# Sliding-window attention and a gated FFN: keys and queries loaded four tokens to a row over all partitions, heads paired two apart

## The chip, the cores and the metric

One core of a Trainium2 chip runs the whole program. The metric is the device time in microseconds (us) of one execution. Engines are called as the profile calls them: PE is TensorE's matmuls, PEld its weight loads, DVE is VectorE, ACT is ScalarE, POOL is GpSimd, SP is SyncE.

## The reference

Attention with sinks and a window over 4 batches, 8 heads, 768 tokens and a head size of 64, followed by a gated FFN over the 3072 tokens:

```python
scores = scale * np.matmul(q, k.transpose(0, 1, 3, 2))
keep = is_sink | in_window            # the first 4 keys, or 0 <= row - col < 128
a = softmax(np.where(keep, scores, -1e9))
attn_out = np.matmul(a, v)
x = attn_out.transpose(0, 2, 1, 3).reshape(B * S, H * D)     # 3072 x 512
g = x @ w_gate                                               # 512 x 1536
out = (g * sigmoid(g) * (x @ w_val)) @ w_out                 # 1536 x 512
```

Inputs and output are float32; the kernel works in bfloat16 with float32 accumulation.

## The kernel before

Tokens are cut into 12 groups of 256, numbered `g`; three groups make a batch, so groups 0, 1 and 2 are batch 0. A group goes through a fixed row of steps: its keys and queries are turned so that the head size lies on the partitions (`kT`, `qT`, two heads stacked on 128 partitions as a pair `p`, the half called `w` or `h`); `step_S` makes scores and their exponentials into the tile `e`; `step_K` and `step_sinks` do the sink keys; `step_PV` multiplies with the values and normalises; `step_X` turns the result for the FFN (`xT`). The FFN runs over eight blocks of 256 or 512 tokens, as `gate` units (a gate projection, a value projection, 6 or 12 per block) and `down` units. The order of all work is written out by hand: the lists given to `weave` put attention steps of later groups between the FFN units of earlier ones. All engines run their own instructions in the program's order.

The keys and queries reach `kT` and `qT` in different ways. Group 0 is cast and turned in `pair_T` (line 572) from the tile `x0`, which holds two tokens of one head in a row. Heads 0 to 3 come as float32 through SP and ACT into the tiles `st` (line 175) and are cast by DVE and ACT (`cast`, lines 562 and 564); heads 4 to 7 come through POOL, cast on the way (line 186). Group 1 comes by `load_rows` (line 100) into `rows`, four tokens of a head in a row, the first head of each pair on partitions 0 to 63 and the second on 64 to 127, and is turned by `step_T` (line 226). Groups 2 and 3 come by `load_nat` (line 111) with one token on each partition and are turned by `step_TN` (line 241). The later groups are turned by DMA (`xbar`).

A turn in `pair_T` and `step_T` is a matmul whose stationary operand is a piece of rows and whose moving operand is the identity `ident`; the outputs for the tokens of one place `r` in the row go to every second or every fourth column of the PSUM tile `pt`.

At the start PE runs 14 matmuls on zeros (`fill`, line 556), then `pair_T(0)`, `pair_T(1)`, `pair_S(0)`, `pair_S(1)`, `pair_T(2)`, `pair_T(3)`, `pair_S(2)`, `pair_S(3)`, the four `step_T` of group 1, `step_PV` of group 0, `step_S` of group 1, and the first gate unit. The loads of group 1, the values and the first gate weights wait in the POOL queue behind those of line 186 (lines 100, 122, 133); POOL also makes `tq` and `tk` (lines 187, 189), from which DVE builds `ident` (line 200). The four `step_TN` of group 2 stand in two FFN units, two in each, at about 25 and 27 us.

`step_vsb` puts the sink values of 8 heads on the partitions where the sink scores of the heads will lie (`load_sinks` gives the order) and masks them with `diag_h`.

Of the kernel before, what the change touches and what calls it, by code (L numbers as in the profile page):

```python
# [7 lines left out]
FP32 = mybir.dt.float32  # L8
BF16 = mybir.dt.bfloat16
AF = mybir.ActivationFunctionType  # L10
ALU = mybir.AluOpType
# [3 lines left out]
def kernel(  # L15
# [12 lines left out]
    nc = tc.nc  # L28
    P = 128
    B, H, S, D = q.shape  # L30
    NS = int(n_sink)
# [7 lines left out]
    NP2 = H // 2  # L39
    GC = S // 256  # L40
# [12 lines left out]
    def pool(name, bufs, psum=False):  # L53
        if psum:
            return ctx.enter_context(
                tc.tile_pool(name=name, bufs=bufs, space=bass.MemoryType.PSUM))
        return ctx.enter_context(tc.tile_pool(name=name, bufs=bufs))

    const = pool("const", 1)
    wpool = pool("wpool", 1)  # L60
    rowp = pool("rowp", 3)
# [16 lines left out]
    def bank(shape, dtype, name):  # L78
        return psum.tile(shape, dtype, tag="b", name=name)


    rows, nats, vas = {}, {}, {}

    def by_rows(src, b, w, pairs, t0):

        hs = slice(2 * pairs.start + w, 2 * pairs.stop, 2)
        return src[b, hs, t0:t0 + 256].rearrange("p (m r) d -> m p (r d)", r=4)

    ALL = slice(0, NP2)

    def new_rows(g):
        rows[g] = rowp.tile([P, 2, NP2, 4 * D], BF16, tag="rows", name="rows")
        return rows[g]

    def load_rows(g, i):
        b, c = divmod(g, GC)
        if g not in rows:
            new_rows(g)
        for w in range(2):
            nc.gpsimd.dma_start(  # L100
                rows[g][64 * w:64 * (w + 1), i],
                by_rows((k, q)[i], b, w, ALL, c * 256))

    def load_nat(g):
        b, c = divmod(g, GC)
# [38 lines left out]
    ident = const.tile([P, P], BF16)  # L144
    mask = const.tile([P, 2, 256], BF16)
    mask0 = const.tile([P, 2, 256], BF16)
    diag_h = const.tile([P, 4], BF16)
    vcf = const.tile([P, 1, D + 1], FP32)
    vcl = const.tile([P, B - 1, D + 1], FP32)
# [15 lines left out]

    def by_two(src, h0, n=4):
        return src[0, h0:h0 + n, 0:256].rearrange("h (m r) d -> m h (r d)", r=2)

    x0 = const.tile([P, 2, H, 2 * D], BF16)
    st = [rowp.tile([P, H, 2 * D], FP32, tag="rows", name="st") for _ in range(2)]
    for h0 in (0, 2):
        for i, eng in ((0, nc.sync), (1, nc.scalar)):
            eng.dma_start(st[i][:, h0:h0 + 2], by_two((k, q)[i], h0, 2))
    nc.scalar.activation(warmed, one, AF.Exp)

    def load_sinks(t, b0, b1):
        for h in range(H):
            r = 32 * (h // 4) + NS * (h % 4)  # L180
            nc.sync.dma_start(
                t[r:r + NS, :, 0:D], v[b0:b1, h, 0:NS].rearrange("b s d -> s b d"))

    load_sinks(vcf, 0, 1)
    for i in range(2):
        nc.gpsimd.dma_start(x0[:, i, 4:8], by_two((k, q)[i], 4))
    nc.gpsimd.iota(tq, [[1, P]], base=0, channel_multiplier=0,
                   allow_small_or_imprecise_dtypes=True)
    nc.gpsimd.iota(tk, [[0, 1]], base=0, channel_multiplier=1,
# [13 lines left out]
    kTs, qTs, es_t, e_t, xns, xTs = {}, {}, {}, {}, {}, {}  # L203
# [7 lines left out]
    def new_T(b):  # L211
        if b not in kTs:
            kTs[b] = kqtp.tile([P, NP2, S], BF16, tag="kT", name="kT")
            qTs[b] = kqtp.tile([P, NP2, S], BF16, tag="qT", name="qT")

    def step_T(g, i, p2, evict=None):
        b, c = divmod(g, GC)
        new_T(b)
        x = rows[g]
        pt = bank([P, 2, 256], FP32, "pt")  # L220
        for pp in range(2):
            p = 2 * p2 + pp
            for r in range(4):
                for w in range(2):
                    h = slice(64 * w, 64 * (w + 1))
                    nc.tensor.matmul(  # L226
                        pt[h, pp, r:256:4], x[h, i, p, r * D:(r + 1) * D],
                        ident[h, h], start=True, stop=True, skip_group_check=True)
        dst = (kTs, qTs)[i][b][:, 2 * p2:2 * p2 + 2, c * 256:(c + 1) * 256]
        if (evict or ("a", "v")[i]) == "a":  # L230
            nc.scalar.copy(out=dst, in_=pt)
        else:
            nc.vector.tensor_copy(out=dst, in_=pt)

    def step_TN(g, i, j, evict="av"):

        b, c = divmod(g, GC)
        new_T(b)
        pt = bank([P, NP2, P], BF16, "pn")
        for p in range(NP2):  # L240
            nc.tensor.transpose(pt[:, p], nats[g][:, i, j, p * P:(p + 1) * P], ident)  # L241
        t0 = c * 256 + j * P
        dst = (kTs, qTs)[i][b][:, :, t0:t0 + P]
        if evict[i] == "a":
            nc.scalar.copy(out=dst, in_=pt)
        else:
            nc.vector.tensor_copy(out=dst, in_=pt)
# [15 lines left out]

    def step_vsb(b):
        vsb = const.tile([P, 4, D + 1], BF16, tag=f"vsb{b}", name="vsb")
        (nc.vector if b else nc.gpsimd).tensor_tensor(
            vsb,
            (vcl[:, b - 1:b] if b else vcf).broadcast_to([P, 4, D + 1]),
            diag_h.rearrange("q (h o) -> q h o", o=1).broadcast_to([P, 4, D + 1]),
            op=ALU.mult)  # L270
        vsbs.append(vsb)

    def step_S(g, p2):
# [50 lines left out]
    def step_sinks(g):  # L324

        b, c = divmod(g, GC)
        for j in range(2):
            for hh in range(2):
                r = slice(32 * (2 * j + hh), 32 * (2 * j + hh + 1))
                pos[j, hh] = bank([P, 4, D + 1], FP32, "o")  # L330
                nc.tensor.matmul(pos[j, hh], es_t[g][r], vsbs[b][r], start=True,  # L331
                                 stop=False, skip_group_check=True)

    def step_PV(g, j, hh, norm="v"):
        b, c = divmod(g, GC)
        t = 2 * c + j
        if hh == 0:
            xns[g, j] = xnp.tile([P, DM], BF16, tag="xn", name="xn")
        if c > 0 and j == hh == 0:
            step_sinks(g)  # L340
        po = pos.pop((j, hh)) if c > 0 else bank([P, 4, D + 1], FP32, "o")
        mms = []
        for hq in range(4):
            h = 4 * hh + hq
            if t > 0:
                vp = vas[g][:, 0, h, 0:D + 1] if j else vas[g - 1][:, 1, h, 0:D + 1]
                mms.append((po[:, hq], e_t[g][:, h, 256 * j:256 * j + P], vp))
            mms.append((po[:, hq], e_t[g][:, h, 256 * j + P:256 * (j + 1)],
                        vas[g][:, j, h, 0:D + 1]))
        for i, (o, l, r) in enumerate(mms):  # L350
            nc.tensor.matmul(o, l, r, start=(c == 0 and i == 0),  # L351
                             stop=(i == len(mms) - 1),
                             skip_group_check=True)

        xn = xns[g, j][:, 256 * hh:256 * (hh + 1)].rearrange("p (h d) -> p h d", h=4)

        def dve():
            rcp = smallp.tile([P, 4, 1], FP32, tag="rcp", name="rcp")
            nc.vector.reciprocal(rcp, po[:, :, D:D + 1])  # L359
            if norm == "a":  # L360
                for hq in range(4):
                    nc.scalar.activation(  # L362
                        xn[:, hq], po[:, hq, 0:D], AF.Copy, scale=rcp[:, hq])
            else:
                nc.vector.tensor_tensor(  # L365
                    xn, po[:, :, 0:D], rcp.broadcast_to([P, 4, D]), op=ALU.mult)
        if norm == "a":
            dve()
        else:
            later.append(dve)  # L370
# [186 lines left out]
                             stop=True, skip_group_check=True)  # L557

    def cast(i, p):
        h = slice(2 * p, 2 * p + 2)  # L560
        if i == 0:
            nc.vector.tensor_copy(out=x0[:, i, h], in_=st[i][:, h])
        else:
            nc.scalar.copy(out=x0[:, i, h], in_=st[i][:, h])

    def pair_T(p):
        new_T(0)
        for i, dst in ((0, kTs[0]), (1, qTs[0])):
            pt = bank([P, 256], FP32, "pt")
            for r in range(2):  # L570
                for w in range(2):
                    nc.tensor.matmul(  # L572
                        pt[64 * w:64 * (w + 1), r:256:2],
                        x0[:, i, 2 * p + w, r * D:(r + 1) * D], ident,
                        start=True, stop=True, skip_group_check=True)
            if p < 2 and i == 0:
                nc.scalar.copy(out=dst[:, p, 0:256], in_=pt)
            else:
                nc.vector.tensor_copy(out=dst[:, p, 0:256], in_=pt)
# [29 lines left out]
    cast(1, 1)  # L609
    nc.vector.tensor_scalar(mask[:, :, P:2 * P], tq2, tk, None, op0=ALU.is_ge)  # L610
    pair_T(0)
    pair_T(1)
    nc.vector.tensor_scalar(sk, tk, float(NS), None, op0=ALU.is_lt)
# [130 lines left out]
```

## Time and profile before

| | |
|---|---|
| median of 3 runs | 238.30 us (237.76, 238.30, 238.68) |
| profiled execution, first to last instruction (span) | 235.8 us |
| mean granted clock over the span | 0.999 |
| PE busy | 229.0 us (97%), 1867 matmuls |
| DVE, ACT, POOL busy | 157.7, 113.6, 74.9 us |
| DMA | 27.62 MB, 108743 packets |

The profile gives the span as the profiled execution's own time; the timed runs are 2.0 to 2.9 us longer, for what lies around the span. In the profile, "L572" is line 572 of the kernel, "pt<-ident,x" an instruction that writes the tile `pt` from `ident` and `x`, and "x16" says how many were merged in one row. A matmul's time in a row includes its way through the array; what a series costs is read from start to start.

### The profile page before, as it was taken

Reading aid. Unit: us, or ns where it says so; the run is one execution under the profiler, and the core shown is the slowest. Engines: PE = TensorE matmul, PEld = TensorE weight load, DVE = VectorE, ACT = ScalarE, POOL = GpSimd, SP = SyncE. Lnnn points to the kernel's source line nnn. Section 1 sums busy time; section 2 is a strip of 40 time slices with the busy share of each in tenths; the row PEclk is TensorE's granted clock in tenths of the full one; section 3 lists DMA queues with packets and bytes.
Section 4 is the critical chain, followed back from the end, with each engine's and each line's share of the span. In section 5 each row is a group of like instructions: output and inputs, shape, how many; then the busy total and the mean of one; then the engine's idle time right before and its main releaser. Section 6 shows DMA issues by size and latency. Waiting matters only on the chain.

```text
span 235.8 us, 4879 instructions
## 1 busy us (share of the span) xinstructions
PE 229.0 (97%) x1867; PEld 127.7 (54%) x1893; DVE 157.7 (67%) x333; ACT 113.6 (48%) x235; POOL 74.9 (32%) x100
## 2 busy tenths in 40 slices
PE   8999999999999999999999999999999999999994
PEld 5768545795555654444445444445444445488443
DVE  4998888768660988950888970698960598877000
ACT  4884495367453826423836522755522653333221
POOL 8995874724403209105325350080000000000000
PEclk9999999999999999999999999999999999999999
DMA  8999999995995929957989997599414100200132
GB/s 138 165 183 176 182 200 204 159 147 81 166 227 164 148 47 88 156 112 160 137 114 133 137 132 185 126 89 101 81 25 150 50 3 0 45 4 0 48 131 91
DMA packets 108743, 27.62 MB, mean 117 GB/s; under 512 B 95792, under 2 KB 105776, under 8 KB 108720
## 3 DMA queue, kind: packets, MB, share of 16 engines
q0 software_dynamic: 76640, 13.90, 76.4%
q1 hardware_dynamic: 30672, 11.58, 25.4%
q10 hardware_dynamic: 1408, 1.84, 2.5%
q8 instruction: 15, 0.25, 0.5%
q14 instruction: 8, 0.07, 0.1%
HBM read 28.34 MB, written 6.29 MB: 147 GB/s over the span
## 4 chain that ended last, share of the span: by engine, by line
PE 93%; DVE 3%; ACT 1%; issue 1%; DVEq 0%; ACTq 0%
PE pv L416 26%; PE pd L496 26%; PE pg L416 26%; PE o L351 4%; PE s L288 4%; PE w L556 1%; DVE xn L365 1%; PE pt L226 1%; PE o L331 1%; PE pt L572 1%; PE pn L241 1%; PE pk L316 1%; ACT th L436 1%; DVE rcp L359 0%; ACT xn L362 0%
## 5 line engine op out<-in xcount | busy, mean ns | idle before, releaser
L444 DVE SCALAR_TENSOR_TENSOR u<-th,pg 128x512 bf16<-128x512 f32 x72 | 49.2, 683 | 39.2 <-ACT th L436 39.2
L416 PE MATMUL pg<-xT,wg 128*128 128x512 bf16 (+1 forms) x353 | 73.5, 336 | 0.7
L436 ACT ACTIVATE th<-pg 128x512 f32<-128x512 f32 x72 | 43.5, 604 | 63.0 <-PE pg L416 58.2
L416 PE MATMUL pv<-xT,wv 128*128 128x512 bf16 (+1 forms) x349 | 72.9, 336 | 0.6 <-ACT e L295 0.2
L496 PE MATMUL pd<-wo,ht 128*128 128x512 bf16 (+2 forms) x292 | 64.5, 371 | 0.5 <-issue 0.2
L416 PEld LDWEIGHTS <-wg 128*128 128x128 bf16 x360 | 35.0, 98 | 27.9 <-issue 0.4
L455 DVE TENSOR_TENSOR ht<-u,pv 128x512 bf16<-128x512 bf16 x62 | 42.7, 688 | 9.4 <-PE pv L416 2.5
L295 ACT ACTIVATE e<-s 128x512 bf16<-128x512 f32 (+1 forms) x88 | 42.8, 581 | 3.9 <-PE s L288 3.7
L496 PEld LDWEIGHTS <-ht 128*128 128x128 bf16 x300 | 27.9, 98 | 30.3 <-issue 0.3
L416 PEld LDWEIGHTS <-wv 128*128 128x128 bf16 x360 | 32.1, 97 | 20.4 <-issue 1.6
L501 ACT ACTIVATE ot<-pd 128x512 f32<-128x512 f32 (+1 forms) x24 | 14.3, 596 | 46.7 <-PE pd L496 40.7
L111 POOL DMA_DIRECT2D nat<-in_k_dram x20 | 17.7, 890 | 39.7 <-DMA qT<-nat 35.8
L300 DVE TENSOR_TENSOR e<-e,mask 128x1024 bf16<-128x1024 bf16 (+1 forms) x44 | 27.2, 653 | 3.7 <-ACT e L295 3.7
L122 POOL DMA_DIRECT2D va<-in_v_dram x24 | 21.5, 919 | 5.5 <-DMA wo<-in_moe_w_out_dram 2.5
L365 DVE TENSOR_TENSOR xn<-o,rcp 128x256 bf16<-128x256 f32 x44 | 18.7, 424 | 1.5
L351 PEld LDWEIGHTS <-e 128*128 128x128 bf16 x352 | 15.0, 98 | 7.9 <-issue 0.2
L111 POOL DMA_DIRECT2D nat<-in_q_dram x20 | 17.7, 899 | 1.1 <-DMA wg<-in_moe_w_gate_dram 0.5
L351 PE MATMUL o<-va,e 128*128 128x65 bf16 x352 | 17.1, 194 | 0.1
L288 PE MATMUL s<-qT,kT 64*128 64x128 bf16 (+1 forms) x240 | 12.9, 238 | 0.0
L288 PEld LDWEIGHTS <-kT 64*128 64x128 bf16 x240 | 7.7, 94 | 7.3 <-issue 6.4
L503 DVE TENSOR_SCALAR ot<-pd 128x128 f32<-128x128 f32 x1 | 0.3, 292 | 14.3 <-PE pd L496 14.3
L359 DVE RECIPROCAL rcp<-o 128x4 f32<-128x4 f32 x48 | 8.3, 175 | 1.0 <-PE o L351 0.9
(74 smaller groups left out, 93.7 us busy)
## 6 DMA issues: line engine op xcount, KB each, us to landing
out_dram<-ot SPq DMA_DIRECT2D x17, 256.0 KB
va<-in_v_dram POOLq DMA_DIRECT2D x24, 128.0 KB, 6.4
nat<-in_k_dram POOLq DMA_DIRECT2D x20, 128.0 KB, 4.4
nat<-in_q_dram POOLq DMA_DIRECT2D x20, 128.0 KB, 5.9
wg<-in_moe_w_gate_dram POOLq DMA_DIRECT2D x6, 256.0 KB, 7.8
wv<-in_moe_w_val_dram POOLq DMA_DIRECT2D x6, 256.0 KB, 8.4
wo<-in_moe_w_out_dram POOLq DMA_DIRECT2D x4, 384.0 KB, 11.1
out_dram<-ot ACTq DMA_DIRECT2D x6, 256.0 KB
```

The costliest lines, as they stand in the source:

```text
L111: nc.gpsimd.dma_start(x[:, i, j].rearrange("p (h d) -> p h d", d=D), src[b, :, t0:t0 + P].rearrange("h p d -> p h d"))
L122: nc.gpsimd.dma_start(va[:, j, :, 0:D], v[b, :, t0:t0 + P].rearrange("h p d -> p h d"))
L288: nc.tensor.matmul(pss[2 * pp + h][:, col:col + n], kTs[b][r, p, kk:kk + P], qTs[b][r, p, qq:qq + n], start=True, stop=True)
L295: nc.scalar.activation(e_t[g][:, h0 + h, lo:512], pss[2 * pp + h][:, lo:512], AF.Exp, scale=scale)
L300: nc.vector.tensor_tensor(e, e, m[:, :, lo:512].broadcast_to([P, 2, 512 - lo]), op=ALU.mult)
L351: nc.tensor.matmul(o, l, r, start=(c == 0 and i == 0), stop=(i == len(mms) - 1), skip_group_check=True)
L365: nc.vector.tensor_tensor(xn, po[:, :, 0:D], rcp.broadcast_to([P, 4, D]), op=ALU.mult)
L416: nc.tensor.matmul(ps[:, i * n:(i + 1) * n], ws[fi][:, c, fo * P:(fo + 1) * P], xTs[tb][:, c], start=(c == 0), stop=(c == DMC - 1))
L436: nc.scalar.activation(th, pg, AF.Tanh, scale=0.5)
L444: nc.vector.scalar_tensor_tensor(u, th, 1.0, pg, op0=ALU.add, op1=ALU.mult)
L455: nc.vector.tensor_tensor(hts[tb][:, f:f + 512 // SIZES[tb]].rearrange("p a n -> p (a n)"), u, pv, op=ALU.mult)
L496: nc.tensor.matmul(po, hts[tb][:, f, ts * P:(ts + 1) * P], wos[f // n][:, f % n, lo:hi], start=(f == 0), stop=(f == DFC - 1))
```

## The change

Batch 0's heads are paired two apart (0 with 2, 1 with 3, 4 with 6, 5 with 7) in place of neighbours. Groups 0 and 1 are loaded with four tokens of one head in a row, and the two heads of a pair alternate from partition to partition, so that each load covers 128 partitions. The number of DMAs stays the same. A turn reads all 128 rows and picks its head by taking every second column of the identity: in `pair_T` there are eight matmuls of 64 columns for four of 128; in `step_T` as many as before, with 128 rows for 64. `step_TN` of group 2 puts its heads into the same pairs, with two transposes of 64 output rows for one of 128. `load_sinks`, `step_vsb` (two POOL operations for one) and `step_PV` follow the new order by `place`.

```diff
+    def by_rows(src, a, t0):
+        return src[0, 4 * a:4 * a + 4, t0:t0 + 256].rearrange(
+            "h (m r) d -> m h (r d)", r=4)
+
+    def place(b, h):
+        return h if b else 4 * (h // 4) + 2 * (h % 2) + h % 4 // 2
...
     def load_rows(g, i):
...
-        for w in range(2):
+        for a in range(2):
             nc.gpsimd.dma_start(
-                rows[g][64 * w:64 * (w + 1), i],
-                by_rows((k, q)[i], b, w, ALL, c * 256))
+                rows[g][:, i, 2 * a:2 * a + 2], by_rows((k, q)[i], a, g * 256))
...
-    x0 = const.tile([P, 2, H, 2 * D], BF16)
-    st = [rowp.tile([P, H, 2 * D], FP32, tag="rows", name="st") for _ in range(2)]
-    for h0 in (0, 2):
+    x0 = const.tile([P, 2, NP2, 4 * D], BF16)
+    st = [rowp.tile([P, NP2, 4 * D], FP32, tag="rows", name="st") for _ in range(2)]
+    for p in range(2):
         for i, eng in ((0, nc.sync), (1, nc.scalar)):
-            eng.dma_start(st[i][:, h0:h0 + 2], by_two((k, q)[i], h0, 2))
+            eng.dma_start(st[i][:, p], (k, q)[i][0, p:p + 3:2, 0:256].rearrange(
+                "w (m r) d -> m w (r d)", r=4))
...
-            r = 32 * (h // 4) + NS * (h % 4)
+            r = 32 * (h // 4) + NS * (place(b0, h) % 4)
...
-        nc.gpsimd.dma_start(x0[:, i, 4:8], by_two((k, q)[i], 4))
+        nc.gpsimd.dma_start(x0[:, i, 2:4], by_rows((k, q)[i], 1, 0))
...
@@ step_T
                     nc.tensor.matmul(
-                        pt[h, pp, r:256:4], x[h, i, p, r * D:(r + 1) * D],
-                        ident[h, h], start=True, stop=True, skip_group_check=True)
+                        pt[h, pp, r:256:4], x[:, i, p, r * D:(r + 1) * D],
+                        ident[:, w:P:2], start=True, stop=True, skip_group_check=True)
@@ step_TN
         for p in range(NP2):
-            nc.tensor.transpose(pt[:, p], nats[g][:, i, j, p * P:(p + 1) * P], ident)
+            x = nats[g][:, i, j]
+            if b:
+                nc.tensor.transpose(pt[:, p], x[:, p * P:(p + 1) * P], ident)
+                continue
+            for w in range(2):
+                h = 4 * (p // 2) + 2 * w + p % 2
+                nc.tensor.transpose(
+                    pt[64 * w:64 * (w + 1), p], x[:, h * D:(h + 1) * D], ident)
@@ step_vsb
-        (nc.vector if b else nc.gpsimd).tensor_tensor(
-            vsb,
-            (vcl[:, b - 1:b] if b else vcf).broadcast_to([P, 4, D + 1]),
-            diag_h.rearrange("q (h o) -> q h o", o=1).broadcast_to([P, 4, D + 1]),
-            op=ALU.mult)
+        sel = diag_h.rearrange("q (h o) -> q h o", o=1)
...
+            for w in range(2):
+                nc.gpsimd.tensor_tensor(
+                    vsb[:, 2 * w:2 * w + 2], vcf.broadcast_to([P, 2, D + 1]),
+                    sel[:, w:4:2].broadcast_to([P, 2, D + 1]), op=ALU.mult)
@@ step_PV
-                mms.append((po[:, hq], e_t[g][:, h, 256 * j:256 * j + P], vp))
+                mms.append((po[:, hq], e_t[g][:, place(b, h), 256 * j:256 * j + P], vp))
...
@@ pair_T
-            for r in range(2):
+            for r in range(4):
                 for w in range(2):
                     nc.tensor.matmul(
-                        pt[64 * w:64 * (w + 1), r:256:2],
-                        x0[:, i, 2 * p + w, r * D:(r + 1) * D], ident,
+                        pt[64 * w:64 * (w + 1), r:256:4],
+                        x0[:, i, p, r * D:(r + 1) * D], ident[:, w:P:2],
                         start=True, stop=True, skip_group_check=True)
```

`cast` takes the pair `p` of `x0` and `st` in one piece, as many columns as before.

## The prediction

> **What bounds the kernel now.** I read the shares of the engines and of the chain first.
>
> ```profile
> PE 229.0 (97%) x1867; PEld 127.7 (54%) x1893; DVE 157.7 (67%) x333; ACT 113.6 (48%) x235; POOL 74.9 (32%) x100
> ...
> PE 93%; DVE 3%; ACT 1%; issue 1%; DVEq 0%; ACTq 0%
> ```
>
> TensorE is the bound, and in the order of time the chain is nearly pure PE from 20.1 us on: whatever the change adds to PE there is added to the end, and whatever moves the first 20 us moves the end as much. So two places count: the head, and the transposes of group 2 (25 to 28 us). The head, from the timeline (start, duration, engine, line):
>
> ```profile
> 1.06 3.17 PE L556 MATMUL w<-zero 128*128 128x256 bf16 x14 [1.06 <-DVE one L161]
> ...
> 1.24 0.89 POOL L186 DMA_DIRECT2D x<-in_k_dram  x1 [0.80 <-POOLq L725]
> ...
> 2.12 0.77 POOL L186 DMA_DIRECT2D x<-in_q_dram  x1
> ...
> 3.22 1.28 POOL L100 DMA_DIRECT2D rows<-in_k_dram  x2
> ...
> 3.55 0.45 DVE L562 CAST x<-st 128x256 bf16<-128x256 f32 x1
> ...
> 4.15 1.92 PE L572 MATMUL pt<-ident,x 128*64 128x128 bf16 x16
> ...
> 6.12 0.42 DVE L579 CAST qT<-pt 128x256 bf16<-128x256 f32 x1 [0.43 <-PE pt L572]
> ...
> 6.87 1.06 PE L572 MATMUL pt<-ident,x 128*64 128x128 bf16 x16
> ...
> 8.66 2.08 DVE L599 TENSOR_TENSOR e<-e,mask 128x768 bf16<-128x768 bf16 x4
> ...
> 9.07 2.08 PE L226 MATMUL pt<-ident,rows 64*64 64x64 bf16 x64
> ```
>
> The first key cast starts at 3.55, 0.02 after its load landed (3.53). PE fills with zero matmuls until about 4.04 and starts turning at 4.15, so it waits 0.1 us for that cast. The first sixteen turns start in pairs 213 ns apart, the second sixteen in pairs 109 ns apart: PE runs at half pace until about 6.4 us. From 6.12 to 14.5 VectorE has almost no gap (evictions, masks, normalisation), and the first gate matmul at 14.74 comes out of it. Turning at 6.87 and 9.07 therefore has some cover, turning at 4.15 has none.
>
> **Loads.** The four first loads were 1,024 packets of 512 B at 27 ns on 16 engines, 1.73 us; they become 512 of 1 KB. Between the 512 B row (27 ns) and the 1,536 B row (68 ns) a 1 KB packet is 47 ns: 1.50 us. So the first lands 0.1 earlier (3.4), the last 0.2 (4.4). The identity, which the turn also needs, ended at 3.64 behind POOL's two L186 issues; with 256 descriptors instead of 512 these take what an L100 issue takes (0.65 each), so it is done by about 3.3. Then the cast ends at 3.9, and what is late next is the fill, ending at 4.04: the turn starts 0.1 earlier, no more. Bounds: 0 (landings do not move) to -0.15.
>
> Queries of heads 4 to 7 landed at 6.86 and are needed at 6.97; they halve from 512 packets of 256 B written to 256 of 512 B. By the rows (239 of the small in 0.5 us, 160 of the large) the two loads save 2.1 - 1.6 = 0.5 us of the GpSimd queue. Behind them: rows of group 1, values, gate weights. None of these holds PE now by more than 0.1 (last query rows landed 10.02, weights loaded at 10.06; wv landed 15.46, used at 15.52), so this is 0.5 us of margin, no time. The number of DMAs on SP, ACT and POOL is the same.
>
> Group 1's rows go to 128 partitions in each DMA instead of 64. They ran at 155 to 169 packets in 0.5 us where the gate weights, over 128 partitions and with the same packet, ran at 167 to 183: about a tenth to gain, also margin. The Trainium skill ("SBUF — State Buffer", section "Door 1: The DMA port swizzle") says that 64 partitions reach half of the ports and get half the bandwidth; by it these loads would be done in half the time. The row shows a tenth, and since their landing is not waited for, the sum is the same by both.
>
> **Turning.** L572 goes from 32 matmuls of 128 columns to 64 of 64 columns, written at a stride of four instead of two; L226 keeps 64 of 64 columns but uses all rows. What is new is a strided identity and full rows at 64 columns. Nearest row: L226 itself, 64 columns at the same output stride, pairs 55.5 ns apart, 27.7 each. Eight of them are 222 ns; the four of 128 columns they replace take 2 x 109 = 218. So zero is taken, in the half-pace stretch too (16 x 107 against 8 x 213). Bounds: if the two column halves streamed at the full rate, pairs at 28 (53 cold), 0.85 us less on the path at 4.15; if the strided identity or the shared rows made the pair take turns, 111 (213 cold), priced below. Thirty-two more weight loads run under the matmuls, as in L226. The Trainium skill ("TensorEngine Tiling (Array Packing)", section "Instruction Overhead") speaks against the change: some 60 cycles of overhead per matmul, so a small free dimension should not be cut. By it, at 2.4 GHz, 32 more matmuls would cost an estimated 0.8 us. The L226 row shows 64 columns at half the price of 128, so I take none.
>
> Evictions keep their shape, 256 columns. Everything behind (VectorE from 6.12) moves by the 0.1.
>
> **Group 2's transposes.** From the timeline of PE:
>
> ```profile
> 25.20 0.61 PE L241 MATMUL pn<-ident,nat 128*128 128x128 bf16 x8
> 25.64 1.03 PE L416 MATMUL pv<-xT,wv 128*128 128x512 bf16 x4
> ...
> 27.37 0.61 PE L241 MATMUL pn<-ident,nat 128*128 128x128 bf16 x8
> ...
> 30.19 0.29 PE L316 MATMUL pk<-qT,kss 128*32 128x128 bf16 x8
> 30.41 1.04 PE L416 MATMUL pv<-xT,wv 128*128 128x512 bf16 x3
> ```
>
> Sixteen transposes in two batches, 56 ns each, nothing lost on either side: same array shape as the gates. They become 32 of 64 output rows each, in two column halves. The trace shows what a change of array shape costs: from the last L316 matmul to L416 151 ns where 56 are the matmul, so 95; L288 to L316 89; L416 to L288 96. Two batches have four such changes: 4 x 93 = 0.37 us on the chain. The transposes themselves: L316's column tiles, contiguous output, start four at once, 66 ns apart, so I let each pair take 56: 4 pairs per step, as before. Upper bound: one after the other, 16 more x 56 = 0.90.
>
> **The rest.** vsb becomes two POOL operations: 0.62 now (14.09 to 14.71), 0.62 to 1.24 then; the sinks use it at 16.69, and the loads of group 2 queued behind it land from 23.76 because the queue, not the issue, is behind. Zero; uncovered, 0.62. The order of heads in the sinks and the e tile costs nothing.
>
> **Sum** on the profiled span: 235.8 - 0.10 + 0 + 0.37 = 236.1. The median of the runs, 238.3, lies 2.5 above the span; 238.6.
>
> **Rivals.** *Column halves of the transposes take turns* (half output rows, one after the other): +0.90, 239.5. For it: L572's pairs need 109 ns for 128 columns, as if serial. Against: L316's tiles run together, and L226, in other rows and columns, is as slow per column as L572, which points to the strided output that both have.
>
> *The turning pair doubles* (strided identity, both halves reading all rows): this is the slower case. Place: 4.15, 6.87 and 9.07. From 4.05 eleven pairs at 213 until the clock rises at 6.4, then five at 111: ends about 7.0 instead of 5.8, +1.2. At 6.87 four groups of 444 ns against VectorE's 335 per eviction: +0.5. At 9.07, 32 pairs at 111 = 3.6 us; its third part is wanted by VectorE at 10.73 and comes about 1.0 late. Sum 2.7, with the 0.37 3.1: 241.4. It decides as soon as a warm pair takes over about 75 ns. No row has a strided moving operand; against it stands that the output stride already halves the pace, which leaves the read time. The Trainium skill's "SBUF" page (same section as above, on 16-byte lines) says two hits to a line suffice, and the strided identity has four.
>
> *The landings set the head after all*: then -0.5 from the queue and -0.1, and with the shape changes falling into waits 237.7; over 0.5% faster only if the pair also runs at its lower bound, 0.85 less: 236.9.
>
> *The loads do not change*: packets stay at 512 B. Then the 0.1 is missing: 238.7, no different.
>
> **Chances.** Forecast 238.6: 0.48. Transposes in turn, 239.5: 0.24, half of it beyond +0.5%. Doubled pair, 241.4: 0.17. Landings or faster turning, 236.9 to 237.7: 0.11, most of it in its lower part. The bound of 0.5%, 1.2 us, is about what a measurement of this kernel can tell from no change. Slower 0.34 (0.17, 0.12, and 0.05 of the forecast where its upper ends, such as an uncovered vsb, come together), faster 0.09, same 0.57. The range leaves out the doubled pair and the lowest case: 237.3 to 240.6.
>
> **What would show it.** Right: L572 at 64 x 64 columns, 1.9 us at 4.05 and 1.06 later; the first key cast near 3.43; L241 of group 2 in batches of 0.44 us with some 93 ns lost on each side; later gates shifted by 0.3. Wrong: L226 taking 3.6 us; the batches taking 0.9; PE waiting for a load before 20 us; or a first gate matmul off 14.64 by over 0.3.

## The result, and the profile after

The changed kernel takes 240.63 us (median of 5 runs, 240.18 to 241.03) against 238.04 us before (5 runs, 237.76 to 238.68): 1.0105 times as long, interval 1.009 to 1.012, or 2.6 us slower. The forecast was 238.6, in a range of 237.3 to 240.6, with the same time as before (0.57) more likely than a slower one (0.34).

The profiled execution is the slowest of the five (241.03 us, span 239.3), and that of before the fastest (237.76, span 235.8), so the two traces lie 3.5 us apart where the medians lie 2.6 apart. The page of the changed kernel, its engines' shares, the granted clock over 40 slices, and the chain by engine and by line:

```profile
PE 230.3 (96%) x1914; PEld 128.4 (54%) x1941; DVE 157.8 (66%) x333; ACT 113.5 (47%) x235; POOL 75.3 (31%) x101
...
PEclk9979999999999999999999999999999999999999
...
PE 89%; DMA 3%; POOL 2%; DVE 2%; issue 2%; ACT 1%; POOLq 0%; DVEq 0%; ACTq 0%
PE pv L428 26%; PE pd L508 26%; PE pg L428 25%; PE s L300 4%; PE o L363 4%; DMA va<-in_v_dram 3%; POOL rows L103 1%; DVE xn L377 1%; PE o L343 1%; PE pk L328 1%; POOL x L186 1%; ACT th L448 1%; PE pn L247 0%; ACT xn L374 0%; PE px L407 0%
```

PE is busy 1.3 us longer, with 47 more recorded matmuls (48 were added: 32 in `pair_T`, 16 in `step_TN`). But its share of the chain fell from 93% to 89%: 3% of the span is now a transfer, the values, and 2% are POOL's issues of loads. In this execution PE waited for loads before 20 us, and the clock has a slice at seven tenths, at 12 to 18 us. The timeline of the head (start, duration, engine, line; in brackets the idle time before and what ended it):

```profile
0.73 1.30 SPq L174 DMA_DIRECT2D st<-in_k_dram  x2
0.74 1.57 ACTq L174 DMA_DIRECT2D st<-in_q_dram  x2
...
1.24 0.82 POOL L186 DMA_DIRECT2D x<-in_k_dram  x1 [0.80 <-POOLq L736]
...
2.05 0.72 POOL L186 DMA_DIRECT2D x<-in_q_dram  x1
...
3.43 0.52 DVE L573 CAST x<-st 128x256 bf16<-128x256 f32 x1
...
4.15 1.06 PE L583 MATMUL pt<-ident,x 128*64 128x64 bf16 x16
...
5.36 0.29 DVE L573 CAST x<-st 128x256 bf16<-128x256 f32 x1 [1.02 <-DMA st<-in_k_dram]
...
5.71 0.89 PE L583 MATMUL pt<-ident,x 128*64 128x64 bf16 x16 [0.49 <-DVE x L573]
5.72 0.40 ACT L575 CAST x<-st 128x256 bf16<-128x256 f32 x1 [1.59 <-DMA st<-in_q_dram]
...
7.38 1.08 PE L583 MATMUL pt<-ident,x 128*64 128x64 bf16 x32
...
9.58 1.98 PE L226 MATMUL pt<-ident,rows 128*64 128x64 bf16 x64
...
13.64 0.62 PE L363 MATMUL o<-va,e 128*128 128x65 bf16 x15 [0.91 <-DMA va<-in_v_dram]
...
14.99 0.76 POOL L280 TENSOR_TENSOR vsb<-vcf,diag_h 128x130 bf16<-128x130 f32 x2
...
16.88 1.89 PE L428 MATMUL pg<-xT,wg 128*128 128x256 bf16 x8
```

In the trace of before, the issues and the first gate matmul stand so:

```profile
0.73 1.04 ACTq L175 DMA_DIRECT2D st<-in_q_dram  x2
0.74 0.97 SPq L175 DMA_DIRECT2D st<-in_k_dram  x2
...
14.74 1.05 PE L416 MATMUL pg<-xT,wg 128*128 128x256 bf16 x8
```

The two float loads of SP now took 1.30 us to issue (before 0.97), those of ACT 1.57 (before 1.04). The casts of the second pair waited 1.02 us (VectorE) and 1.59 us (ScalarE) for them, and PE, which had no gap there before, stood idle from the last turn of the first pair, begun at 4.87, to 5.71: 0.84 us from start to start where the pairs before it follow in 0.11, so 0.73 us too long (the 0.49 in the row counts from the modelled end of the last turn). In the trace the four float loads landed at 3.32, 3.61, **5.33 and 5.70**; before at 3.53, 3.79, 4.32 and 4.61. The first pair came 0.2 earlier, the second 1.0 later.

From there the lateness against the trace of before grows: first turn 0.0, group 1's turns (L226) 0.5, last `px` of the first half block 1.5 (15.29 against 13.75), first gate 2.1 (16.88 against 14.74), sinks matmul 3.0 (19.65 against 16.69), first transpose of group 2 3.1 (28.26 against 25.20), scores of group 2 3.4 (33.06 against 29.64), end 3.5. Nearly all arises before 20 us, from 0.5 on with a wait for the values (0.91) and a stretch at half clock: the first gate matmuls take 1.89 where they took 1.05, and over 15.4 to 18.8 the granted clock is 0.50 of full speed ("half clock" from here on). The row of that window (stretch, busy PE and matmuls, granted clock, DMA share, GB/s):

```profile
15.40:18.80 3.40, 3.40 (x32) 0.50 1.60 190
```

Group 2, later in the same timeline, is where the rest lies:

```profile
28.26 0.64 PE L247 MATMUL pn<-ident,nat 128*64 128x128 bf16 x16
28.83 1.04 PE L428 MATMUL pv<-xT,wv 128*128 128x512 bf16 x4
29.70 1.03 PE L428 MATMUL pg<-xT,wg 128*128 128x512 bf16 x4
30.66 0.64 PE L247 MATMUL pn<-ident,nat 128*64 128x128 bf16 x16
```

Sixteen transposes of 64 output rows take 0.64 us in a row, little more than the 0.61 of eight with 128. The column halves run together, 56 ns a pair. From the first of them to the scores of group 2 it is 4.80 us against 4.44: 0.36 more.

### The profile page after: what moved, and what is told of

It reads as the page before. It is cut to its first block, busy times and chain, and to the rows that moved or that the text cites. A ratio compares the mean times of both kernels' runs of the same rounds, so it can differ in the third digit from the quotient of the medians.

```text
span 239.3 us, 4975 instructions
## 1 busy us (share of the span) xinstructions
PE 230.3 (96%) x1914; PEld 128.4 (54%) x1941; DVE 157.8 (66%) x333; ACT 113.5 (47%) x235; POOL 75.3 (31%) x101
## 4 chain that ended last, share of the span: by engine, by line
PE 89%; DMA 3%; POOL 2%; DVE 2%; issue 2%; ACT 1%; POOLq 0%; DVEq 0%; ACTq 0%
PE pv L428 26%; PE pd L508 26%; PE pg L428 25%; PE s L300 4%; PE o L363 4%; DMA va<-in_v_dram 3%; POOL rows L103 1%; DVE xn L377 1%; PE o L343 1%; PE pk L328 1%; POOL x L186 1%; ACT th L448 1%; PE pn L247 0%; ACT xn L374 0%; PE px L407 0%
```

## Experiments

Four theories at first. *Instruction supply*: the changed kernel's added PE instructions drew an instruction transfer forward (the first of 16 KB ran at 11.34, before at 13.41), and that delayed the values. *Group 2's column halves* cost what the shapes cost, 0.37. *POOL's loads* in between made the second float loads late. *The clock*: the waits led to the half pace at 15.4. Later, *the form of the float loads themselves*. Each ratio below is to the kernel before, measured beside the run (medians 238.04 to 238.11), with its 95% interval.

**e1.** In the kernel before, 32 more matmuls (64 more PE instructions, with their weight loads) ahead of everything, with the same number of columns.

```diff
-    fill(14, bank([P, 512], FP32, "w"))
+    fill(46, bank([P, 512], FP32, "w"), 78)
```

> The kernel before, with the 14 zero matmuls of 256 columns at the start cut into 46 of 78 columns: the same number of columns, but 64 more instructions on PE, as many as the change adds to the head; nothing else differs. Theory (instruction supply): the first 16 KB transfer of the instruction queue comes earlier, at about 11.3 us after the span's start in place of 13.4, one sixteenth of the second half of the values (va) waits behind it and lands after 12.8 us in place of 11.8, PE waits for it 0.7 to 1.1 us, and the time rises by 1.0 to 2.5 us. Rival (the values are late because of the new load pattern alone): the transfer may move, but the values land at 11.8 +- 0.3 and the time stays within 0.4 us of before.

Measured: 238.18 us (11 runs), ratio 1.0008 (0.9996 to 1.002). The instruction transfer moved to 12.35 and the values landed at 11.93 (before 11.76). The count of PE instructions isn't the cause. A transfer as early as 11.34 was not reproduced here, but the traces of e3, e4 and f5 below show that the loss does not need it: there the transfer ran at 13.69, 14.77 and 14.51, after the values had landed (11.72, 12.46, 12.39), and the medians are 240.3 to 241.3 all the same.

**e2.** In the kernel before, group 2's transposes alone in two halves, the old pairs kept.

```diff
         for p in range(NP2):
-            nc.tensor.transpose(pt[:, p], nats[g][:, i, j, p * P:(p + 1) * P], ident)
+            if b:
+                nc.tensor.transpose(pt[:, p], nats[g][:, i, j, p * P:(p + 1) * P], ident)
+                continue
+            for w in range(2):
+                h = 2 * p + w
+                nc.tensor.transpose(
+                    pt[64 * w:64 * (w + 1), p], nats[g][:, i, j, h * D:(h + 1) * D], ident)
```

> The kernel before, with group 2's transposes alone made in two column halves (32 of 64 output rows in place of 16 of 128), in the old pairs. Theory (four changes of array shape at 93 ns, pairs 56 ns apart): +0.4 us, 238.4. Rival (the halves take turns): +1.3 us. Rival (hidden): 0.

Measured: 238.72 us (11 runs), ratio 1.0027 (1.0015 to 1.0039), which is 0.36 to 0.93 us. In the trace the stretch from the first transpose to the scores takes 4.80 (26.02 to 30.82), as in the changed kernel. The trace gives 0.36, as predicted (0.37), which is the lower end of what the runs allow.

**e3.** In the changed kernel, POOL's two loads of line 186 behind the iotas, so that they come later.

```diff
-    for i in range(2):
-        nc.gpsimd.dma_start(x0[:, i, 2:4], by_rows((k, q)[i], 1, 0))
     nc.gpsimd.iota(tq, [[1, P]], base=0, channel_multiplier=0,
...
+    for i in range(2):
+        nc.gpsimd.dma_start(x0[:, i, 2:4], by_rows((k, q)[i], 1, 0))
```

> The changed kernel with POOL's two iotas ahead of its two first loads, so that these are issued 0.45 us later; nothing else differs. In the changed kernel the second float loads land at 5.33 and 5.70 where before they landed at 4.32 and 4.61. Theory (they wait because POOL's loads now reach the DMA engines at 3.05 in place of 3.66 and run in front of them): they land at 4.7 +- 0.2 and 5.0, the second cast moves up from 5.36, and up to 0.5 us comes back. Rival (the issuing path makes this pattern's descriptors slowly): they land at 5.2 to 5.4 as in the changed kernel, and the time is that of the changed kernel.

Measured: 240.33 us (4 runs), ratio 1.0099 (1.0076 to 1.0122), no better than the changed kernel. The loads were issued only 0.12 later (1.36), too little a change to decide on it; the second float loads landed at 5.34 and 6.69.

**e4.** In the changed kernel, nine zero matmuls ahead of the wait for the values.

```diff
     step_S(1, 0)
+    fill(9, bank([P, 512], FP32, "w"))
     masks1 = list(later)
```

> The changed kernel with 9 zero matmuls of 256 columns (about 1 us) between the scores of group 1's first half and the value products of group 0's second half, where PE waits for the values. They change no result. Theory (the idle PE before 15.4 us brings the stretch at half pace from 15.4 to 18.8 us, worth 1.4 us): the stretch goes, the granted clock is 0.999, the first gate matmuls run at 109 ns each, and the time falls by 1.0 to 1.4 us. Rival (PE is not the limit in that stretch): the clock is 0.999 and the time stays within 0.4 us of the changed kernel. If the clock still falls, other idle time brings it.

Measured: 241.25 us (6 runs, 239.43 to 242.71), ratio 1.0125 (1.0086 to 1.0165): nothing came back. In this profiled execution the values landed at 12.46 and PE did not wait for them, but it stood still for 1.4 us at 4.87, since the second float loads landed at 5.61 and 5.94, and the granted clock rose from half to full only at 9.87. So the wait at 4.87 is common to the traces of the changed kernel, e3 and e4, and that for the values is not; the next runs go to the float loads.

**f3.** In the changed kernel, only the float loads back to two tokens a row, the pairs still two apart, and the first two turns in the form that this needs.

```diff
-            eng.dma_start(st[i][:, p], (k, q)[i][0, p:p + 3:2, 0:256].rearrange(
-                "w (m r) d -> m w (r d)", r=4))
+            eng.dma_start(
+                st[i][:, p].rearrange("m (w e) -> m w e", w=2),
+                (k, q)[i][0, p:p + 3:2, 0:256].rearrange("w (m r) d -> m w (r d)", r=2))
```

> The changed kernel with the four float loads alone put back to two tokens in a row (512 B pieces, a token pair on each of 128 partitions, turned as before); the pairs two apart, POOL's loads, the rows of group 1 and group 2's halves stay as changed. If the float loads in their new form are the cause (theory 2), the second ones land at 4.4 +- 0.2, the wait at 4.9 goes, and the time is 238.4 to 239.0, what is left being group 2's 0.36. If POOL's larger pieces are the cause (theory 1), they land after 5.0 and the time stays at 240.0 to 240.8.

Measured: **238.26 us** (11 runs, 238.05 to 239.03), ratio 1.0013 (1.0002 to 1.0023), a little under the 238.4 to 239.0 expected. Its timeline:

```profile
0.73 1.04 ACTq L174 DMA_DIRECT2D st<-in_q_dram  x2
0.74 0.97 SPq L174 DMA_DIRECT2D st<-in_k_dram  x2
...
4.15 1.92 PE L585 MATMUL pt<-ident,x 128*64 128x128 bf16 x16
...
6.89 1.08 PE L591 MATMUL pt<-ident,x 128*64 128x64 bf16 x32
...
14.73 1.05 PE L429 MATMUL pg<-xT,wg 128*128 128x256 bf16 x8
```

The issues are short again, the loads land at 3.29, 3.52, 4.02 and 4.86, PE turns without a gap, and the first gate matmul starts at 14.73 (before 14.74). Line 591 is the changed kernel's own turn with the strided identity, and it costs no time. What is left over the kernel before, 0.2 us by the medians (0.05 to 0.55 by the ratio), agrees with group 2's 0.36: its stretch takes 4.81. Of the 2.6 us, 2.4 (240.63 less 238.26) are the float loads' form.

**g3.** The converse: in the kernel before, the second pair of float loads issued later, on ACT behind the load of the activation table, on SP behind three loads of sinks.

```diff
     for h0 in (0, 2):
         for i, eng in ((0, nc.sync), (1, nc.scalar)):
             eng.dma_start(st[i][:, h0:h0 + 2], by_two((k, q)[i], h0, 2))
-    nc.scalar.activation(warmed, one, AF.Exp)
...
-    load_sinks(vcf, 0, 1)
+        if h0 == 0:
+            nc.scalar.activation(warmed, one, AF.Exp)
+            load_sinks(vcf, 0, 1, range(3))
+    load_sinks(vcf, 0, 1, range(3, H))
```

> The kernel before with its second float loads made late by their place in the queues alone: on ACT behind the table load, on SP behind three of the eight sink loads; nothing else differs. They should land at 5.2 to 6.2 in place of 4.3 and 4.6, as in the changed kernel. Theory (late second float loads, with PE idle at 4.9, are the loss of the change): the time rises by 1.5 to 2.5 us to 239.6 to 240.6. Rival (the loss needs the other parts of the change): less than 0.8 us.

Measured: 240.58 us (6 runs, 240.09 to 241.91), ratio 1.0115 (1.0087 to 1.0143), 2.5 us slower with nothing changed but the order of these issues. Its timeline, and its windows (columns as above):

```profile
6.41 0.34 DVE L563 CAST x<-st 128x256 bf16<-128x256 f32 x1 [2.02 <-DMA st<-in_k_dram]
...
6.80 0.63 PE L573 MATMUL pt<-ident,x 128*64 128x128 bf16 x8 [1.75 <-DVE x L563]
```

```profile
5.00:7.00 2.00, 0.25 (x6) 1.00 1.57 190
8.20:11.50 3.30, 3.30 (x32) 0.50 1.95 174
```

Only the keys were late, by about 2 us (issued at 2.34, cast at 6.41); the queries' load went out at 1.31 all the same. PE had 0.25 us of work in 2 us, and after it came a stretch of half clock, from 8.16 to 11.57. The delay is not that of the change (one load 2 us late in place of two 1 us late), but a late float load alone does what the change did, and by the same picture: idle PE, then half pace.

**f4.** In the changed kernel, four zero matmuls between the first and the second pair's turns: the wait stays, PE is busy in it.

```diff
     pair_T(0)
+    fill(4, bank([P, 512], FP32, "w"))
     pair_T(1)
```

> The changed kernel with 4 zero matmuls of 256 columns between the first pair's turns and the second's, where PE waits for the second float loads; they change no result and cost nothing while that wait is 0.8 us or more. Theory (the idle at 4.9 shifts or undoes the clock's rise, and in most runs half pace from 15 us on is its consequence): the clock rises at 4.5 to 6.6 us, stays, and the time falls to 239.3 to 239.8. Rival (the clock has no part): 240.3 to 240.8.

Measured: 239.18 us (5 runs, 238.93 to 239.7), ratio 1.0047 (1.0031 to 1.0062): 1.45 us come back, although the loads landed as late as ever (5.89 and 6.06).

```profile
5.15 1.03 PE L568 MATMUL w<-zero 128*128 128x256 bf16 x4
...
6.26 0.69 PE L583 MATMUL pt<-ident,x 128*64 128x64 bf16 x16
...
15.58 1.05 PE L428 MATMUL pg<-xT,wg 128*128 128x256 bf16 x8
```

The second pair turns at 6.26, later than without the fill (5.71); the clock rose at 6.41 and stayed. The mean clock is 0.998 to 1.0 in all five runs, against 0.993 in four of five of the changed kernel. (This mean leaves out the time before the first rise: f5's profiled run has 1.000, though its clock rose only at 10.45.) The first gate is 0.84 later than before, group 2 adds 0.36: 1.20, where the runs show 1.1. So of the 2.6 us some 0.8 are the lateness itself (the fill's own delay included) and 0.36 the shapes; the other 1.45 exist only when PE stands idle in that wait.

Three runs ask why the new loads are late.

**f5.** POOL's loads of line 186 back to two tokens a row (and the turns of heads 4 to 7 with them), the float loads as changed.

```diff
-        nc.gpsimd.dma_start(x0[:, i, 2:4], by_rows((k, q)[i], 1, 0))
+        nc.gpsimd.dma_start(
+            x0[:, i, 2:4].rearrange("m a (w e) -> m (a w) e", w=2),
+            (k, q)[i][0, 4:8, 0:256].rearrange("h (m r) d -> m h (r d)", r=2))
```

> The changed kernel with POOL's two loads of group 0 alone put back to two tokens in a row (512 pieces of 256 B written, turned as before); the float loads stay as changed. Theory 1 (POOL's larger and earlier pieces hold back the float loads): the second float loads land at 4.4 +- 0.3 and the time is 238.5 to 239.2. Theory 2 (the float loads in their new form are slow by themselves): they land at 5.0 to 5.7 and the time is 240.3 to 241.0, with POOL's queue 0.5 us later.

Measured: 240.4 us (6 runs, 239.02 to 240.82), ratio 1.0079 (1.0051 to 1.0108). The second float loads landed at 6.22 and 6.39, PE stood still from 4.87 to 6.59, and the clock rose at 10.45. The form of POOL's loads is not what delays them.

**f1.** POOL's loads only after the float loads have landed (two tiny POOL copies read `st` first), so that nothing runs beside those.

```diff
+    for i in range(2):
+        nc.gpsimd.tensor_copy(out=late, in_=st[i][0:1, 1, 0:1])
     for i in range(2):
         nc.gpsimd.dma_start(x0[:, i, 2:4], by_rows((k, q)[i], 1, 0))
```

> The changed kernel with POOL's iotas first and then two tiny POOL copies that read the second float tiles, so that POOL's own loads are issued only when the float loads have landed. The whole head becomes later by some 2 to 3 us; what counts is when the second float loads land (5.33 and 5.70 in the changed kernel, 4.32 and 4.61 before). Theory 1 (POOL's loads run in front of them on the DMA engines): they land at 4.2 +- 0.3 and 4.5 +- 0.3. Theory 2 (the issuing path of SP and ACT is slow with two heads to alternate partitions): at 5.0 to 5.7 still.

Measured, one run: 242.97 us, since heads 4 to 7 came late, as intended. The issues stayed at 0.58 to 0.88 us each, and the second float loads landed at 4.76 and 4.96. That lies between the two theories: about 0.4 later than before without any load of POOL's beside them, where with POOL's loads it is 1.0 or more. The packets of these second loads, 128 to each, ran over 1.0 and 1.3 us; in g1 below, 128 packets of the same size ran over 0.65 and 0.69. So the new form is slow by itself in this one run, and the rest comes with POOL's loads, whose packets run from 3.05 on in the changed kernel's trace (3.66 before) and get in between. That earlier start goes with the form of the float loads and not with POOL's own: with POOL's old form it is 3.02 (f5), with the old form of the floats 3.40 (f3).

**g1.** The float loads with as large pieces (1 KB) over as many partitions (128), but all from one head: 512 tokens of one head in place of 256 of two.

```diff
-            eng.dma_start(st[i][:, p], (k, q)[i][0, p:p + 3:2, 0:256].rearrange(
-                "w (m r) d -> m w (r d)", r=4))
+            eng.dma_start(st[i][:, p], (k, q)[i][0, p, 0:512].rearrange(
+                "(m r) d -> m (r d)", r=4))
```

> The changed kernel with the float loads taking 128 rows of 1 KB from one head (its first 512 tokens) where they take 64 rows of each of two heads: as many bytes and pieces of the same size, into the same place, but the source steps through 128 rows as the destination steps through 128 partitions. Heads 0 to 3 of group 0 are computed from the wrong tokens, so only the times count. Theory (it is the two-heads-to-alternate-partitions form that SP and ACT issue slowly): an issue takes 0.45 to 0.52 us in place of 0.66 to 0.88, and the second loads land at 4.3 +- 0.3. Rival (pieces of 1 KB, however laid out, are behind POOL's loads): issues as short, landing 5.2 to 6.2. Rival (the number of rows per instruction): issues 0.6 to 0.9 and landing 5.2 to 6.2.

Measured, one run: 238.62 us.

```profile
0.73 0.90 ACTq L174 DMA_DIRECT2D st<-in_q_dram  x2
0.74 0.87 SPq L174 DMA_DIRECT2D st<-in_k_dram  x2
...
4.07 1.28 PE L583 MATMUL pt<-ident,x 128*64 128x64 bf16 x32
```

The issues took 0.39 to 0.46 us, shorter than those before the change, the loads landed at 3.44, 3.66, 4.08 and 4.28, and all 32 turns follow in one row, from 4.07. The time is 0.5 over before: group 2's 0.36, and group 1's rows, which the earlier PE now waited for at 8.87 (0.36). Pieces of 1 KB are what the prediction took them for. What is slow is the pattern in which the source comes as 64 rows by 2 heads and goes to 128 partitions in alternation; which of the two, no run separates.

**g2.** The last run looked for a version better than both: f3 with the four `step_TN` of group 2 in one unit, which saves two changes of shape.

```diff
-        (4, TN(2)[::2]), (5, TN(2)[1::2]), ((6, 7), Ss(2)), (6, [K(2)]),
+        (5, TN(2)), ((6, 7), Ss(2)), (6, [K(2)]),
```

> The kernel with the float loads put back to two tokens in a row (238.26 measured), and group 2's four transposing steps in one FFN unit in place of two, so that the array's shape changes twice in place of four times. Theory (93 ns for each change of shape): 0.19 us less, 238.1, level with the kernel before. Rival (the evictions of four steps in one unit hold PE up): 238.3 to 238.8.

Measured: 238.57 us (12 runs, 238.1 to 240.51), ratio 1.0035 (1.0013 to 1.0058). The theory had 238.1. It is not better than f3 or the kernel before; five of its runs lie between 239.3 and 240.5, and why is open. No version here beats the kernel before.

## Why the prediction was wrong

The measured 240.63 lies at the upper edge of the range, 0.03 beyond it, and that it lies so near is luck: the edge was drawn for transposes in turn and for upper ends such as an uncovered vsb, and neither came. Two of the prediction's own signs of being wrong did come: PE waited for a load before 20 us, and the first gate matmul stood at 16.88, 2.2 off the 14.64.

**The failed step** is in the part on loads: "so the first lands 0.1 earlier (3.4), the last 0.2 (4.4)", and the bound on it, "0 (landings do not move) to -0.15". The first half held (3.32). The last landed at 5.70. The working went from packet durations alone; what feeds the packets was taken as unchanged because the number of DMAs was. The issue rows of SP and ACT, which the trace of before has (0.45 to 0.52 us each), were not costed for the new pattern: they became 0.58 to 0.88. The packets show it too. Before, SP's second load began with the next packet behind the last of the first (2.89 after 2.88); after, it began at 3.24 where the last of the first had started at 2.89, and its packets were strewn over 1.7 us. A gain was allowed for the unknown pattern, a loss was not, and no row excluded it. By f3 this one term is 2.4 us where the sum had -0.1. Its price was large because the prediction's own reading was right: "turning at 4.15 has none", no cover.

**The rival that was missing.** Late landings were weighed only as an upside ("the landings set the head after all", faster). The slower case was given to the turning pair, which did not double: pairs of L583 start 106 ns apart at half clock and 52 to 56 at full clock, and 64 matmuls of 64 columns cost what 32 of 128 did. A strided identity is free here, and so the estimate of 0.8 us for 32 more matmuls falls as well.

**The clock** came into no step. The sum let a late load cost its lateness. f4 shows that in this place, before and around the rise of the clock, an idle PE costs more than its idle time: 1.45 of 2.6 us went when it was kept busy. The Trainium skill ("TensorE: Matmul & The Clock Gate", section "HAM oscillation — how this bites in real kernels") asks for no idle gap of PE beyond some 3.4 us. These runs are stricter: in g3 a wait of 2.1 us was followed by 3.41 us at half clock, and in the changed kernel's profiled execution no two matmuls started more than 1.12 us apart ahead of it and 3.41 us at half clock still came. In these traces it is not the single gap alone that counts. The stretches of the clock between its first rise and the last microseconds are whole multiples of 3.41 us (10.24, then 3.41 at half, in the changed kernel), and in the 3.41 us ahead of a drop to half clock PE was busy for 1.96 in the changed kernel (11.97 to 15.38), 1.62 in g3 and 1.99 in f1. Before the change it was 3.13 or more in each such stretch of the head, and 2.17 in e3 kept full clock too. In e4 and f5 the clock did not rise at 6.46 and 7.04, behind 2.31 and 2.03 us of PE work in 3.41, but one stretch later. No limit can be read from this: near the end of g3 a stretch with 1.78 was followed by full clock.

**What held.** Group 2: +0.37 predicted, +0.36 in all nine traces with the halves in two units, the column halves together; "transposes in turn" (+0.90) falls. The two vsb operations took 0.76 us within the predicted 0.62 to 1.24, hidden. That the head shifts the end one for one held in f4 (0.84 at the first gate and 0.36 of group 2, against 1.14). Without the loads' term the sum is 238.04 + 0.37 = 238.4, and f3 measured 238.26.

**Smaller misses.** The turn did not start 0.1 earlier, though the first cast began at 3.43 as predicted and was done at 3.95. The reading that PE waits 0.1 us for that cast was wrong: in f1 the cast was done at 3.43, and the turn still began at 4.15. In both, as before, the last zero matmul starts at 3.80 and the first turn 0.35 behind it. POOL's issues did not shrink to 0.65: the two of line 186 took 0.82 and 0.72 (before 0.89 and 0.77), and each load of rows 0.72 for 0.65, so the values' first issue went back from 5.7 to 6.0 us where 0.5 us of margin had been counted.

**Open.** Why that one pattern is issued and fed more slowly; how the 1.45 us divide in a given execution between late values, a late rise of the clock (9.87 and 10.45 in e4 and f5) and a later half-clock stretch (e3 and e4 did not separate them); and how the changed kernel's run of 240.93 lost its time at a mean clock of 0.999 (a late first rise, as in f5, would not show in that mean; no trace here shows that run).

## What to carry to other kernels

A load has three prices: its issue, the supply of its pieces, and the pieces themselves; larger pieces lower the last, and the pattern that makes them can raise the first two, so ask of a new pattern whether source and destination still step alike, and where the first work of the kernel waits for it, let the bound reach to both sides. Where such a wait can't be avoided in the first microseconds, keep PE busy through it: four zero matmuls gave back more than half of the loss.

## What the runs showed of the hardware

- A float32 load of two heads' 64 rows of 1 KB onto alternating partitions took 0.58 to 0.88 us to issue on SP or ACT; 128 rows of 1 KB of one head 0.39 to 0.46; 256 pieces of 512 B, two to a partition, 0.45 to 0.52. The Trainium skill ("DMA: Bandwidth & Descriptors", section "Issuing engines are not separate DMA queues") calls the sequencer's time to initiate a DMA usually small beside the DMA itself; here 0.58 to 0.88 us of issue stand beside packets that ran 0.65 to 0.69 us from first to last where nothing held them up (g1).
- A matmul of 64 columns in one column half, output at a stride of four, moving operand at a stride of two: 52 to 56 ns a pair at full clock, the same as with a contiguous identity (55.5), and 106 at half clock.
- The granted clock first rose between 3.9 us (g1) and 6.7 us (g2) in the other traces that record it, and at 9.9 and 10.5 us in the two where PE had stood idle for 1.4 and 1.7 us at 4.87 (e4, f5). A stretch of half clock lasted 3.41 us in the changed kernel and in g3, which is the 0.007 that a mean clock of 0.993 lacks, and 6.83 in f1, whose PE waited for loads from 6.5 to 8.8 and from 9.1 to 10.6 us.
